# GpSimd's loads in another order, in a kernel for windowed attention and channel mix

## The chip, the cores and the metric

The kernel runs on one core of a Trainium2 chip. The metric is the device time of one execution in microseconds (us), the median of several runs. Five engines work side by side, each through an instruction list of its own: TensorE (PE; PEld are its weight loads), VectorE (DVE), ScalarE (ACT), GpSimd (POOL) and SyncE (SP). Data move by DMA. SP, ScalarE and GpSimd issue DMAs, each on a queue of its own.

## The reference

Eight batches, eight heads, 576 positions, 64 values per head. Causal attention in a window of 128 positions with a linear bias by distance is followed by a channel mix (a feed-forward step with a shift by one position):

```python
scores = q @ k.T / 8 + slope_h * -|i - j|        # masked to 0 <= i - j < 128
x      = softmax(scores) @ v                     # heads side by side: 512 columns
x_prev = x shifted down by one position
xk, xr = mu * x + (1 - mu) * x_prev              # with mu_k and mu_r
out    = sigmoid(xr @ w_r) * (relu(xk @ w_k) ** 2 @ w_v)    # 512 -> 1024 -> 512
```

Inputs and output are float32; the kernel computes in bfloat16 and accumulates in float32.

## The kernel before, in words

All work is written down as nodes of a plan: each has an engine, a duration that the author supposes, dependencies, a priority, the buffers that it takes and gives back, and a function that emits the instruction. `Plan.run` plays the plan through in time. On each engine it takes the ready node with the smallest key that gets its buffers. The order so found is the order in which the instructions are issued. The supposed times decide the order and nothing else; on the chip, an instruction waits for what it really needs, and in each engine's list nothing passes a waiting instruction.

The work on TensorE, by the line numbers of the profile:

- `warm` (L654): 90 matmuls on zeros, with the last priority. They fill TensorE's time at the start when nothing else is ready in the plan.
- q and k are transposed to have the head dimension on partitions: batch 0's first 256 positions from float32 stages (L1097, L1100), the rest with four quarter-array transposes at a time (`qk_quad`, L1053; `halves`, L804). All of them need `ident`, an identity that DVE makes (L408) from `dist`, which GpSimd fills by iota (L404). Two selects on GpSimd (L412, L415) then cut `dist` to the window, and DVE copies it.
- `tails` (L906, L879) does the same for positions 512 to 575.
- `scores` (L693, for batch 0 and the first steps after it with a bias matmul, L680), then exp on ScalarE (L707); later batches multiply by a mask on DVE (L720).
- `attend` (L749) multiplies by v, with a column of ones for the sum; DVE divides (L755, L760).
- The result is transposed back (`out_t` L787, `out_some` L804, for the last two batches by DMA), and `shift` makes xk and xr on DVE (L847, L854).
- `channel_mix`: K (L958, `wk_sb`), relu on ScalarE (L965), the square on DVE (L931) or, in the first three chunks, on DVE or ScalarE (L929), R (L976, `wr_sb`) with a tanh on ScalarE (L983), V (L992, `wv_sb`), the product on DVE (L997), and the store on SP (L1022). The last row block is made in two pieces of 384 and 128 columns; the second is stored by ScalarE (L1016).

The loads: batch 0's first part comes on SP's and ScalarE's queues (`first_load`, L517). All else is loaded and cast to bfloat16 by GpSimd's DMAs, in the order of the text, set by `LOADS = 'vK23tVkabRcWw'` and then by a, b, c for each of the batches 2 to 7. v and V are the halves of batch 0's v, K and k those of w_k, 2 and 3 batch 0's q and k from position 256 on (heads 0 to 3 and 4 to 7), t its tails, R is w_r, W and w are the halves of w_v, and a, b, c are q and k, the tails, and v of a batch. Each of GpSimd's DMAs in the plan depends on the one before it (`last.get(queue)`).

In the plan, each transfer also takes time on one shared resource (`fab`): its bytes by a rate, times a factor by kind (`COST`). Keys of attention nodes come from `rank`: a step number less a lead interpolated from `LEAD`, plus a shift by step kind from `SHIFT`. On TensorE, `pe_key` prefers work of the array shape that is set up, if that is the half-height one (`rows` 64), and can put quarter-array transposes (`lazy`) back by `WAIT`, which is 0.

Of the kernel before, what the change touches and what calls it, by code (L numbers as in the profile page):

```python
# [33 lines left out]
class Plan:  # L34
# [148 lines left out]
def kernel(  # L183
# [14 lines left out]
    B, H, S, D = q.shape  # L198
# [26 lines left out]
    PART_WIDE = True  # L225
    QK1 = (ACT, DVE)
    TW = (0,)
    QUAD = 0.040
# [7 lines left out]
    COST = {'first': 1.28, 'v': 1.15, 'q': 0.944, 'ts': 0.66, 'tv': 0.58, 'w': 0.88, 'run4': 1.0, 'run2': 1.03, 'flip': 1.0, 'mu': 1.0, 'x': 1.0}  # L236
    SS = ()
    OH = range(1, 6)
    QM = 2
# [16 lines left out]
    VDEP = 1  # L256
    TCOST = 1.5
    KLAST = 1

    def XT(b, g):  # L260
        return (ACT,) if b else XT0
# [68 lines left out]
    def dve_t(n, fast=1):  # L330
# [1 line left out]

    AHEAD = 30.0
    LEAD = {
        PE: (46.3, 80.42, 22.29, 25.79, 41.56, 20.38, 22.23, 21.29, 23.26, 26.51),
        ACT: (-27.56, -45.55, 35.23, -5.26, -38.06, -61.17, 26.65, -81.7, -33.31, -34.13),
        DVE: (-18.77, -31.64, -26.58, 23.63, -67.49, 40.6, 13.9, -0.29, -44.69, 6.99),
    }
    KNOTS = range(-4, 36, 4)
    SHIFT = {  # L340
        PE: {(0, 0): 84.89, (1, 0): -15.49, (2, 0): 37.21, (3, 0): 68.05, ('fkk',): -41.42, ('p1', 'fkk'): 6.29, ('p1', 'fxk'): 4.19},
        ACT: {(1, 0): -163.12, (2, 0): 31.31, (3, 0): 165.14, ('frl',): 21.61, ('rl', 'fp1'): 159.69, ('rs', 'fp1'): -160.42},
        DVE: {(0, 0): -143.93, (1, 0): 53.57, (1, 1): -50.21, (1, 2): -15.35, (2, 0): 32.09, (3, 0): -4.67, ('fp1', 'frs'): -48.4, ('frl',): -99.03, ('ot', 'fp1', 'frs'): -1.01},
    }
    NBIAS = 4
    XRL = 4.0
# [1 line left out]
    SLOPE = 4.7  # L348
# [6 lines left out]
    def rank(prio, need, free):  # L355

        if prio[0] == 0:
            _, b, part, g = prio[:4]
            k = 4 * b + g if b or part else g - 4
            step = (prio[4] if len(prio) > 4 else 9, prio[5] if len(prio) > 5 else 0)  # L360
            return {e: ((k - lead(e, min(k, 32))) * SLOPE + SHIFT[e].get(step, 0.0),) + tuple(prio)
                    for e in LEAD}
        if prio[0] == 1:
            what = tuple(sorted(h.cls for h in need)) + tuple(
                "f" + c for c in sorted({h.cls for h in free}))
            return {e: (prio[1] + SHIFT[e].get(what, 0.0),) + tuple(prio) for e in LEAD}
        return {e: (1e9,) + tuple(prio) for e in LEAD}

    def op(e, dur, deps, prio, emit, need=(), free=()):
# [190 lines left out]
    def load_step(what):  # L560
        if what in "vV":
            if what == "v" and VCUT:
                n_w["d"] = pool_op(0.55, emit_cut, [n_ident])
            for j in ((0, 1) if what == "v" else (2, 3)):
                vl[0].append(v_load(0, j, vh[0], [gv[0]] + blank_v + (
                    src0[1, VDEP - 1] if VDEP and j == 0 else [])))
                if j == 0 and not VCUT:
                    n_w["d"] = pool_op(0.55, emit_cut, [n_ident, last[POOL]])
                    last[POOL] = n_w["d"]
            if what == "V":  # L570
                vl[0].append(tv_load(0, vh[0], blank[0:4]))
# [28 lines left out]
    def batch_load(b, what):  # L600
        if what == "a":
            ch[b] = Hold("cb")
            g_ = virtual("cb", [ch[b]])
            if b not in WIDE:
                cl[b] = full_load(b, 0, ch[b], g_) + full_load(b, 1, ch[b], g_)
            else:
                cw[b] = [wide_load(b, ch[b], g_, 4 * j, 4 * j + 4) for j in range(2)]
        elif what == "b":
            th[b], tl[b] = tail_load(b)
            if b in XB:  # L610
                xbh[b] = Hold("qx")
                g_ = virtual("qx", [xbh[b]])
                xbl[b] = [flip(b, i, j, g_) for i in range(2) for j in range(NF)]
            if b in XTT:
                tail_flip(b)
        elif what == "c":
            vh[b] = Hold("vs")
            gv[b] = virtual("vs", [vh[b]])
            vl[b] = [v_load(b, j, vh[b], [gv[b]]) for j in range(NF)]
            vl[b].append(tv_load(b, vh[b]))  # L620

    for what in LOADS:
        load_step(what)
    n_dist, n_wr = n_w["d"], n_w["r"]
    n_wk = [n_w["k", 0], n_w["k", 1]]
    n_wv = [n_w["v", 0], n_w["v", 1]]
    for b in range(2, B):
        for what in "abc":
            batch_load(b, what)

    n_copy = {}
# [260 lines left out]
    def tails(b, prio):  # L892
        htt = Hold("tt")
        hs = th[b]
        if b in XTT:
            plan.follow(last["tt"], ttg[b])
            last["tt"] = ttg[b]
            return tth[b], ttl[b]
        if b not in TW:
            return tails_full(b, prio, htt, hs)  # L900
        hp = Hold("p1")

        def emit(e):
# [8 lines left out]
        t = op(PE, 0.03 * 16, list(tl[b]) + [n_ident], prio + (0,), emit, [hp], [hs])  # L912
        g = virtual("tt", [htt])
# [29 lines left out]
    def channel_mix(P, c0, c1, first, xks, xrs, order):  # L943
# [27 lines left out]
        for i, c in enumerate(range(c0 // 128, c1 // 128)):  # L971
# [30 lines left out]
            for a, b in ((0, FIN), (FIN, 512)) if final else ((0, 512),):  # L1002
# [42 lines left out]
    def qk_quad(b, g, nr, buf, deps, prio, c0, hq, take, free):  # L1045
# [3 lines left out]
        def emit(e):  # L1049
            for n in range(2 * nr):  # L1050
# [8 lines left out]
        t.rows, t.lazy = (64, 64), True  # L1059
# [241 lines left out]
```

## Time and profile before

| | us |
|---|---|
| median of 3 runs (lowest, highest) | 232.38 (231.59, 232.47) |
| the profiled execution | 232.61 |
| its span, first to last instruction | 230.8 |
| TensorE busy | 221.1 (96%) |
| VectorE busy | 186.9 (81%) |
| ScalarE busy | 163.9 (71%) |
| GpSimd busy | 93.7 (41%) |

The granted TensorE clock is full throughout. In lines of the profile, the first number of a timeline row is the start in us, the second its length, and xN the number of instructions that were merged. Of a wait, "A <- B: total, times, longest" says that A stood still until B had ended. For GpSimd, the time of a DMA row is that of its issue, not of the transfer.

### The profile page before, as it was taken

The numbers are of one execution on the slowest core, as the hardware profiler recorded it, in microseconds if no ns is written. First come the engines' busy times: TensorE is split into PE (matmuls) and PEld (weight loads), VectorE is DVE, ScalarE is ACT, GpSimd is POOL, SyncE is SP. The second block draws the span as 40 slices with busy tenths as digits, with TensorE's granted clock in tenths as the row PEclk, the third lists the DMA queues.
The fourth block names the chain that finished last, engine by engine and source line by source line (L and its number), as shares of the span: only waits on it lengthen the run. The fifth ranks groups of instructions, "written<-read, shape, count | busy, mean of one in ns | idle before, by whom it ended". The sixth has DMA issues, their size and how long they took to land.

```text
span 230.8 us, 6660 instructions
## 1 busy us (share of the span) xinstructions
PE 221.1 (96%) x2682; PEld 134.3 (58%) x2715; DVE 186.9 (81%) x422; ACT 163.9 (71%) x296; POOL 93.7 (41%) x120
## 2 busy tenths in 40 slices
PE   7999998899999999999999999999999999999993
PEld 7575765665665755545665755545655654455562
DVE  7495998799977999899769998979999999343342
ACT  3769999489999977898897776964847516417260
POOL 8786655579869950686001990070000000000000
PEclk9999999999999999999999999999999999999999
DMA  6999999999999999989962999499723222121222
GB/s 169 182 163 194 189 158 200 200 167 151 201 147 169 171 125 167 119 82 175 227 98 70 179 151 206 93 122 169 128 57 121 67 82 76 46 92 45 69 70 91
DMA packets 121566, 31.11 MB, mean 135 GB/s; under 512 B 108216, under 2 KB 117696, under 8 KB 121536
## 3 DMA queue, kind: packets, MB, share of 16 engines
q0 software_dynamic: 96016, 16.26, 97.8%
q1 hardware_dynamic: 23776, 13.84, 25.1%
q10 hardware_dynamic: 1744, 0.59, 1.1%
q8 instruction: 21, 0.34, 0.6%
q14 instruction: 9, 0.07, 0.1%
HBM read 33.56 MB, written 9.44 MB: 186 GB/s over the span
## 4 chain that ended last, share of the span: by engine, by line
PE 77%; DMA 16%; issue 2%; POOL 2%; DVE 1%; ACT 1%; DVEq 0%; POOLq 0%; ACTq 0%
PE uno L992 25%; PE uno L958 25%; PE uno L976 12%; DMA wk_sb<-in_moe_w_k_dram 7%; PE duo L749 6%; PE duo L693 5%; DMA cb<-in_k_dram 5%; DMA vs<-in_v_dram 4%; PE uno L804 3%; POOL vs L467 1%; PE uno L1053 0%; DVE dl L847 0%; POOL tv L472 0%; PE uno L879 0%; ACT xt L663 0%
## 5 line engine op out<-in xcount | busy, mean ns | idle before, releaser
L958 PE MATMUL uno<-xk,wk_sb 128*128 128x256 bf16 (+2 forms) x413 | 70.8, 313 | 0.6 <-ACT qk L663 0.4
L992 PE MATMUL uno<-wv_sb,kk 128*128 128x512 bf16 (+2 forms) x282 | 69.5, 373 | 1.9 <-issue 0.8
L707 ACT ACTIVATE at<-duo 128x1024 bf16<-128x1024 f32 (+2 forms) x68 | 65.1, 1002 | 6.1 <-PE duo L693 5.3
L965 ACT ACTIVATE rl<-uno 128x256 bf16<-128x256 f32 (+2 forms) x104 | 47.4, 487 | 30.2 <-PE uno L958 27.0
L958 PEld LDWEIGHTS <-wk_sb 128*128 128x128 bf16 x416 | 38.5, 98 | 22.4 <-issue 0.4
L467 POOL DMA_DIRECT2D vs<-in_v_dram x32 | 28.5, 908 | 45.3 <-PE duo L749 37.2
L992 PEld LDWEIGHTS <-kk 128*128 128x128 bf16 x296 | 27.0, 98 | 27.7 <-issue 1.2
L720 DVE TENSOR_TENSOR at<-at,mask 128x1024 bf16<-128x1024 bf16 x56 | 37.3, 681 | 3.4 <-ACT at L707 3.4
L931 DVE TENSOR_TENSOR kk<-rl 128x256 bf16<-128x256 bf16 (+2 forms) x96 | 30.9, 336 | 9.9 <-ACT rl L965 8.8
L997 DVE SCALAR_TENSOR_TENSOR ot<-rs,uno 128x512 f32<-128x512 bf16 (+2 forms) x37 | 24.4, 667 | 13.8 <-PE uno L992 10.3
L976 PE MATMUL uno<-wr_sb,xr 128*128 128x512 bf16 x128 | 34.3, 379 | 0.8
L983 ACT ACTIVATE rs<-uno 128x512 bf16<-128x512 f32 x36 | 22.2, 628 | 11.7 <-PE uno L976 11.7
L663 ACT COPY qk<-uno 128x512 bf16<-128x512 bf16 (+1 forms) x42 | 22.6, 605 | 5.1 <-PE uno L1053 3.7
L854 DVE SCALAR_TENSOR_TENSOR xr<-dl,mu_sb,xt 128x576 bf16<-128x576 bf16 (+1 forms) x32 | 24.6, 777 | 0.0
L854 DVE SCALAR_TENSOR_TENSOR xk<-dl,mu_sb,xt 128x576 bf16<-128x576 bf16 (+1 forms) x32 | 24.3, 778 | 0.0
L760 DVE TENSOR_TENSOR xu<-duo,rc 128x640 bf16<-128x640 f32 x28 | 22.5, 813 | 2.1 <-PE uno L804 2.1
L749 PEld LDWEIGHTS <-at 128*128 128x128 bf16 x576 | 21.1, 98 | 5.1 <-issue 0.5
L976 PEld LDWEIGHTS <-xr 128*128 128x128 bf16 x144 | 13.6, 98 | 14.2 <-issue 0.2
L498 POOL DMA_DIRECT2D cb<-in_q_dram x20 | 17.7, 916 | 5.6 <-PE uno L804 3.2
L749 PE MATMUL duo<-vs,at 128*128 128x65 bf16 x448 | 18.7, 194 | 0.1
L498 POOL DMA_DIRECT2D cb<-in_k_dram x20 | 17.7, 916 | 2.2 <-PE uno L804 1.6
L663 ACT COPY xt<-uno 128x640 bf16<-128x640 bf16 (+3 forms) x28 | 15.1, 580 | 3.8 <-PE uno L804 2.4
(83 smaller groups left out, 200.3 us busy)
## 6 DMA issues: line engine op xcount, KB each, us to landing
out_dram<-ot SPq DMA_DIRECT2D x30, 256.0 KB, 4.1
vs<-in_v_dram POOLq DMA_DIRECT2D x32, 128.0 KB, 7.0
cb<-in_q_dram POOLq DMA_DIRECT2D x20, 128.0 KB, 6.1
cb<-in_k_dram POOLq DMA_DIRECT2D x20, 128.0 KB, 5.5
out_dram<-ot SPq DMA_DIRECT2D x10, 128.0 KB, 1.8
wk_sb<-in_moe_w_k_dram POOLq DMA_DIRECT2D x2, 512.0 KB, 7.5
cb<-in_q_dram POOLq DMA_DIRECT2D x4, 256.0 KB, 10.0
cb<-in_k_dram POOLq DMA_DIRECT2D x4, 256.0 KB, 10.4
```

Of the source, the lines that this page charges most:

```text
L467: return dma(POOL, 256, issue_t(1024), lambda e: nc.gpsimd.dma_start(out=vs_buf[h.idx][:, j, :, 0:D], in_=v[b, :, 128 * j:128 * j + 128].r ...
L498: return [dma(POOL, 256, issue_t(1024), lambda e, r=r: nc.gpsimd.dma_start(out=cb_buf[h.idx][:, i, r], in_=src[:, :, r]), [g], kind="q") f ...
L663: (nc.scalar.copy if e == ACT else nc.vector.tensor_copy)(out=out, in_=in_)
L707: lambda e, ah=ah, w=w, hp=hp: nc.scalar.activation(out=ah(), in_=two(hp)[:, :, 0:w], func=AF.Exp, scale=float(scale)), (), [hp])
L720: nc.vector.tensor_tensor(out=a, in0=a, in1=m, op=ALU.mult)
L749: nc.tensor.matmul(a[:, hl, t - t0], lhsT=at[:, lo:lo + 128], rhs=vs[:, u, 2 * g + hl, :] if u < NF else tvb[:, 2 * g + hl], start=(u == u ...
L854: lambda e: nc.vector.scalar_tensor_tensor(out=buf[hk.idx][:, g, e0 + c0:e0 + c1], in0=dls(), scalar=mu[:, g:g + 1], in1=xc(1), op0=ALU.mu ...
L931: nc.vector.tensor_tensor(out=out, in0=in_, in1=in_, op=ALU.mult)
L958: nc.tensor.matmul(one(hp)[:, 0:n], lhsT=wk_sb[:, po, 128 * fo:128 * fo + 128], rhs=xk_buf[hx.idx][:, po, c0:c1], start=(po == 0), stop=(p ...
L965: a = op(ACT, act_t(n), [s], pr, lambda e, hp=hp, hr=hr: nc.scalar.activation(out=rl_buf[hr.idx][:, 0:n], in_=one(hp)[:, 0:n], func=AF.Rel ...
L976: nc.tensor.matmul(one(hp), lhsT=xr_buf[hx.idx][:, po, 128 * c:128 * c + 128], rhs=wr_sb[:, po], start=(po == 0), stop=(po == NPO - 1))
L992: nc.tensor.matmul(one(hv)[:, a:b], lhsT=kk_buf[hk.idx][:, fo, o:o + 128], rhs=wv_sb[:, fo, a:b], start=(fo == 0), stop=(fo == NFO - 1))
```

## The change

The change keeps every instruction's work and moves instructions. `order` means the issue order on an engine.

1. GpSimd's DMAs no longer depend on each other in the plan (`PFREE`). Each gets a key: its place in the text plus a number for its group (`PKEY`; the group is the batch and the letter). A load whose buffer is not free yet lets later ones pass. The iota and the selects take part in this, with their place as key.
2. In the plan, the transfer of 37 early loads takes a time of its own from a table (`LAND`), in place of bytes by rate.
3. `rank` adds shifts for batches 0 and 1 by step (`FIRST`), by head pair (`PAIR`) and by what a feed-forward node takes and gives (`MIX`); `LEAD`, `SHIFT` and `QUAD` have new numbers, and `WAIT` is 13.59.
4. `pe_key` tells three array shapes apart in place of one: 64 (scores), 63 (`qk_quad`) and 127 (`tails`).
5. The five row blocks whose store is issued in two halves begin one block earlier: the last but one is stored whole (`CUTOFF`).
6. Tail loads of v name the hold of v as a dependency.

In the new program GpSimd's list begins: q of heads 0 to 3 ('2'), the two tail loads ('t'), k of heads 0 to 3, both loads of 'v', 'K', then the iota, q of heads 4 to 7 ('3'), the two selects, k of heads 4 to 7, 'V', then 'a' and 'b' mixed, 'R', 'k', three loads of 'c', 'W', the other two of 'c', batch 2's first load, 'w', batch 2's other three, four tail loads, and so on. Of the filler matmuls, 58 stand ahead of the first real one (30 before) and 32 behind it. ScalarE's list has 7 squares more.

```diff
     def pe_key(self, n, rows):
         key = n.prio["PE"] if isinstance(n.prio, dict) else n.prio
-        if rows == 64 and n.rows[0] == 64:
+        if rows < 128 and n.rows[0] == rows:
             return (-1e8,) + tuple(key)
...
-    WAIT = 0.0
+    WAIT = 13.59
...
+    LAND = {
+        '0v1': 1.03, '0K0': 2.27, '020': 0.73, '021': 0.77, '030': 0.75, '031': 0.9, '0t0': 0.75,
...
+    CUTOFF = 2
+    PFREE = True
...
+            def at(e):
+                s = (k - lead(e, min(k, 32))) * SLOPE + SHIFT[e].get(step, 0.0)
+                if b < 2:
+                    s += FIRST[e].get((b, part) + step, 0.0) + PAIR[e].get((b, part, g), 0.0)
+                return s
+            return {e: (at(e),) + tuple(prio) for e in LEAD}
...
-        us *= COST.get(getattr(n, "kind", None), 1.0)
+        us = LAND.get(getattr(n, "load", None), us * COST.get(getattr(n, "kind", None), 1.0))
...
+    PKEY = {
+        '0v': -8.52, '0K': -7.98, '02': -0.25, '03': -25.82, '0t': -61.35, '0V': -5.2, '0k': 6.38,
...
     def dma(queue, kb, issue, emit, deps=(), need=(), free=(), lat=(1.0, 0.9), flip=False, kind='x'):
-        n = plan.add(queue, issue, 0.0, list(deps) + [last.get(queue)],
-                     (len(plan.nodes),), emit, need)
+        free_ = PFREE and queue == POOL
+        n = plan.add(queue, issue, 0.0, list(deps) + ([] if free_ else [last.get(queue)]),
+                     (PKEY.get(group[0], 0.0) + place[0], len(plan.nodes)) if queue == POOL else (len(plan.nodes),),
+                     emit, need)
...
     def pool_op(dur, emit, deps=()):
-        n = plan.add(POOL, dur, 0.2, list(deps) + [(last.get(POOL), 0.0)],
-                     (len(plan.nodes),), emit)
+        n = plan.add(POOL, dur, 0.2, list(deps) + ([] if PFREE else [(last.get(POOL), 0.0)]),
+                     (place[0] - 0.5, len(plan.nodes)), emit)
...
-                        cut = (a, 256, b) if 0 < B * S - 128 - row <= 128 * n_split else (a, b)
+                        cut = (a, 256, b) if 128 * CUTOFF <= B * S - 128 - row < 128 * (n_split + CUTOFF) else (a, b)
```

More of the change, by code (lines that the diff above doesn't have):

```diff
@@ L227 @@
     TW = (0,)
-    QUAD = 0.040
+    QUAD = 0.035
     RUN = {2: 64 * 284 / 345.0, NF: 128 * 284 / 390.0}
@@ L234 @@
     NO = 5
-    WAIT = 0.0
-    COST = {'first': 1.28, 'v': 1.15, 'q': 0.944, 'ts': 0.66, 'tv': 0.58, 'w': 0.88, 'run4': 1.0, 'run2': 1.03, 'flip': 1.0, 'mu': 1.0, 'x': 1.0}
+    WAIT = 13.59
+    COST = {
+        'first': 1.28, 'v': 1.15, 'q': 0.94, 'ts': 0.66, 'tv': 0.58, 'w': 0.88, 'run4': 1.0, 'run2':
+        1.03, 'flip': 1.0, 'mu': 1.0, 'x': 1.0,
+    }
+    LAND = {
[6 rows of a table added]
+    }
     SS = ()
@@ L340 @@
     SHIFT = {
-        PE: {(0, 0): 84.89, (1, 0): -15.49, (2, 0): 37.21, (3, 0): 68.05, ('fkk',): -41.42, ('p1', 'fkk'): 6.29, ('p1', 'fxk'): 4.19},
-        ACT: {(1, 0): -163.12, (2, 0): 31.31, (3, 0): 165.14, ('frl',): 21.61, ('rl', 'fp1'): 159.69, ('rs', 'fp1'): -160.42},
-        DVE: {(0, 0): -143.93, (1, 0): 53.57, (1, 1): -50.21, (1, 2): -15.35, (2, 0): 32.09, (3, 0): -4.67, ('fp1', 'frs'): -48.4, ('frl',): -99.03, ('ot', 'fp1', 'frs'): -1.01},
+        PE: {
+            (0, 0): 99.96, (1, 0): 4.2, (2, 0): 27.32, (3, 0): 102.83, ('fkk',): -6.62, ('p1',
+            'fkk'): 0.33, ('p1', 'fxk'): -1.01,
+        },
+        ACT: {
+            (1, 0): -298.05, (2, 0): 77.7, (3, 0): 214.26, ('frl',): -106.04, ('rl', 'fp1'): 54.43,
+            ('rs', 'fp1'): -149.39,
+        },
+        DVE: {
+            (0, 0): -148.98, (1, 0): 70.65, (1, 1): -77.21, (1, 2): -53.91, (2, 0): 78.03, (3, 0):
+            0.86, ('fp1', 'frs'): -66.8, ('frl',): -42.09, ('ot', 'fp1', 'frs'): -49.77,
+        },
+    }
+    FIRST = {
+        PE: {
[3 rows of a table added]
+        },
+        ACT: {
+            (0, 0, 3, 0): -12.01, (0, 0, 2, 0): -1.6, (0, 0, 1, 0): 1.62, (0, 1, 3, 0): 10.66, (0,
+            1, 2, 0): -19.23, (0, 1, 1, 0): 49.91, (1, 0, 3, 0): -27.16, (1, 0, 2, 0): 30.91, (1, 0,
+            1, 0): -23.81,
+        },
+        DVE: {
[4 rows of a table added]
+        },
+    }
+    PAIR = {
+        PE: {
[3 rows of a table added]
+        },
+        ACT: {
[3 rows of a table added]
+        },
+        DVE: {
[6 rows of a table added]
+        },
+    }
+    MIX = {
+        PE: {
+            (0, 'p1', 'fxk'): 63.56, (0, 'p1', 'fkk'): -28.77, (0, 'fkk'): -13.61, (1, 'p1', 'fxk'):
+            -14.46, (1, 'p1', 'fkk'): -12.63, (1, 'fkk'): -45.13,
+        },
+        ACT: {
+            (0, 'rl', 'fp1'): 16.16, (0, 'frl'): -36.53, (0, 'rs', 'fp1'): -32.31, (1, 'rl', 'fp1'):
+            -35.06, (1, 'frl'): -9.5, (1, 'rs', 'fp1'): -83.25,
+        },
+        DVE: {
+            (0, 'frl'): 52.11, (0, 'ot', 'fp1', 'frs'): 55.27, (1, 'ot', 'fp1', 'frs'): -26.97, (1,
+            'frl'): 8.37,
+        },
     }
@@ L365, in rank @@
                 "f" + c for c in sorted({h.cls for h in free}))
-            return {e: (prio[1] + SHIFT[e].get(what, 0.0),) + tuple(prio) for e in LEAD}
+            return {e: (prio[1] + SHIFT[e].get(what, 0.0) + (
+                MIX[e].get((prio[2] // 14,) + what, 0.0) if prio[2] < 28 else 0.0),) + tuple(prio)
+                    for e in LEAD}
         return {e: (1e9,) + tuple(prio) for e in LEAD}
@@ L390, in fab @@
         return x
-    def dma(queue, kb, issue, emit, deps=(), need=(), free=(), lat=(1.0, 0.9), flip=False, kind='x'):
-        n = plan.add(queue, issue, 0.0, list(deps) + [last.get(queue)],
-                     (len(plan.nodes),), emit, need)
+    PKEY = {
[5 rows of a table added]
+    }
+    group, place = [""], [0.0]
+    def dma(queue, kb, issue, emit, deps=(), need=(), free=(), lat=(1.0, 0.9), flip=False, kind='x'):
+        free_ = PFREE and queue == POOL
+        n = plan.add(queue, issue, 0.0, list(deps) + ([] if free_ else [last.get(queue)]),
+                     (PKEY.get(group[0], 0.0) + place[0], len(plan.nodes)) if queue == POOL else (len(plan.nodes),),
+                     emit, need)
+        if queue == POOL:
+            place[0] += 1
+            n.group = group[0]
+            n.load = group[0] + str(sum(1 for x in plan.nodes if getattr(x, 'group', None) == group[0]) - 1)
         n.kind = 'flip' if flip else kind
@@ L619, in batch_load @@
             vl[b] = [v_load(b, j, vh[b], [gv[b]]) for j in range(NF)]
-            vl[b].append(tv_load(b, vh[b]))
+            vl[b].append(tv_load(b, vh[b], [gv[b]]))
     for what in LOADS:
+        group[0] = "0" + what
         load_step(what)
@@ L628 @@
         for what in "abc":
+            group[0] = str(b) + what
             batch_load(b, what)
```

13 lines of the change are left out of this document (6 added, 7 removed), and 28 rows, old and new, of tables (FIRST, LAND, PAIR, PKEY).

## The prediction

> **What bounds the kernel now.** First the page. Its PE line says that TensorE is busy for 221.1 of 230.8 us, so a better order can win only the rest, plus what TensorE does without need. Second, TensorE's waits, once whole and once from 53 us on:
>
> ```profile
> PE uno L654 <- DVE warm L434: 1.0, 1, 1.0
> PE uno L992 <- DMA wv_sb<-in_moe_w_v_dram: 0.7, 1, 0.7
> PE duo L680 <- ACT at L707: 0.5, 1, 0.5
> PE uno L958 <- ACT qk L663: 0.4, 1, 0.4
> PE uno L1097 <- DMA qx<-in_q_dram: 0.3, 1, 0.3
> PE uno L1053 <- DMA cb<-in_k_dram: 0.3, 1, 0.3
> PE uno L1100 <- ACT qk L663: 0.2, 1, 0.2
> PE uno L1053 <- ACT qk L663: 0.2, 1, 0.2
> PE uno L749 <- ACT xt L663: 0.2, 1, 0.2
> ```
>
> After 53 us the same view holds one line, 0.6 us in four pieces of 0.2. So a rearranged middle can win at most 0.6 us; what can be won lies ahead of 53 us and behind TensorE's end (227.3). Third, the timeline of TensorE's first microseconds, and GpSimd's beside it:
>
> ```profile
> 0.99 3.27 PE L654 MATMUL uno<-warm 128*128 128x128 bf16 x30 [0.99 <-DVE warm L434]
> 4.10 0.56 PE L1100 MATMUL uno<-ident,qx 128*128 128x128 bf16 x4
> ```
> ```profile
> 0.84 0.34 POOL L404 IOTA dist<- 128x256 bf16 x1 [0.39 <-POOLq L1285]
> ...
> 2.22 2.00 POOL L467 DMA_DIRECT2D vs<-in_v_dram  x2
> 4.21 0.76 POOL L508 DMA_DIRECT2D wk_sb<-in_moe_w_k_dram  x1
> 4.96 0.76 POOL L463 DMA_DIRECT2D qx<-in_q_dram  x1
> 5.69 0.77 POOL L463 DMA_DIRECT2D qx<-in_k_dram  x1
> ...
> 7.89 0.67 POOL L482 DMA_DIRECT2D ts<-in_q_dram  x1
> 8.52 0.65 POOL L482 DMA_DIRECT2D ts<-in_k_dram  x1
> ```
>
> Real work begins at 4.10. It needs `ident`, which DVE makes from the iota that GpSimd finishes at 1.18. The 90 filler matmuls (L654) do no work. Fourth, ScalarE: the table of stretches has it busy 10.00 of 10 us from 30 to 40, and then it idles:
>
> ```profile
> 39.75 1.02 ACT L707 ACTIVATE at<-duo 128x1024 bf16<-128x1024 f32 x1
> 43.91 1.56 ACT L663 COPY qk<-uno 128x512 bf16<-128x512 bf16 x3 [3.14 <-PE uno L1053]
> ```
>
> It waits for transposes of batch 2, and these for k of batch 2 (landed 43.5). The page's DMA row is full over the first 40 us. The front is thus shared between loads and ScalarE.
>
> **What TensorE loses ahead of 53 us now.** 0.99 at the start, 3.3 for 30 fillers, 60 x 0.056 = 3.4 for the later ones (13 of them took 0.89 us, the last one's 0.22 included), and the waits of the list without its first line, 2.8: together 10.5 us.
>
> **1. The start.** In the instruction order of the new program GpSimd issues, ahead of the iota, one q load of part 2, the two tail loads, one k load, two v loads and half of wk. From the first free moment of GpSimd (0.84) and start to start: 2 x 0.73 (4.96 to 5.69) + 2 x 0.64 + 2.00 + 0.75 = 5.5, so the iota starts at 6.3. From the iota's start to that of `ident` are 0.57 (0.84 to 1.41), and `ident` takes 0.13: the first real transpose stands at 7.1 instead of 4.10, **3.0 us late**. On DVE three casts of first loads now stand ahead of `ident`; the last wants k of head pair 1, which landed at 4.6, so 2 us may go before that decides. Queued behind the iota are one more q load and the two selects; with 0.73 and 0.64 they end at 8.1, and the distance copies on DVE by 8.5. The first bias matmul (L680) is due then: 7.1 + transposes 2 x 0.33 + 12 fillers 0.7 = 8.4. So this costs nothing more.
>
> The fillers stand 58 ahead of that transpose and 32 behind it (30 and 60 before). The 58 end at 0.99 + 3.3 + 28 x 0.056 = 5.9 and TensorE then idles 1.2. The later ones cost 32 x 0.056 = 1.8 instead of 3.4. New loss: 7.1 + 1.8 = **8.9 us plus its waits w**. Without any wait that wins 1.6 us; w = 1.6 is the break-even.
>
> **2. The loads.** GpSimd's stream begins 1.4 us earlier (0.84 instead of 2.22). Its data do not begin as soon: in the DMA view of the first 5 us only SP's and ScalarE's queues move data (0.80 MB), and GpSimd's have no packet, although its first load was issued at 2.22. So the stream gains between 0.4 us (it has to share with the first loads, and delays them) and 1.4 (it does not). The row is that no packet was seen while the other two queues were full. [...]
>
> wv's first half, which ended the 0.7 us wait, now has batch 1's last v block and v tail behind it instead of ahead: 384 KB at the 180 to 190 GB/s of the table of stretches, 2.0 us. It lands 2.4 to 3.4 us earlier, near 34.5. Batch 2's second load keeps the same set ahead and gains 0.4 to 1.4 (near 42.5), while 36 AV matmuls, 8 of K, 4 of V and 20 output transposes are put ahead of its first transposes: 36 x 0.031 + 8 x 0.109 + 4 x 0.216 + 0.4 = 3.2 us more of other work. The DMA waits (0.7, 0.3, the 0.3 of the first loads) and the 0.4 behind the batch 2 copy go: **1.7 off the waits**, and ScalarE's 3.14 us hole mostly closes.
>
> **3. What is late next: ScalarE.** It starts 3 us later. Of batch 0's and 1's first three feed-forward chunks it gets 7 more squares (0.32 each back to back, 43 to 37 and 29 to 28 on DVE) two 512-wide copies less (0.48) and one 256-wide more (0.31): +1.6 us. To offset that it had about 4 us of idle time between 4.69 and 15.7, of which the earlier part 2 fills some, and the 3.14 hole. The four ScalarE waits above were 1.1 us (0.5 + 3 x 0.2). Bounds for w: 0 (they are filled as well) and 4 (a 3 us late start and 1.6 more work, less the 0.6 or so that could be filled at once). I take 1.0, by the row it is nearest to, the four waits of now. Front: 8.9 + 1.0 - 10.5 = **-0.6**.
>
> **4. The middle.** In both programs TensorE changes its array shape 118 times and runs the same matmuls, so new keys and the two new modes only permute. Later batches' tail loads go ahead of v and of q, k. Batch 3's q and k landed at 59.2, their first transposes ran at 62.2: about 3 us of cover against two tail loads pulled ahead (1.2 us each at 47 us). Value 0, between -0.6 (the list) and +1.5 (cover gone).
>
> **5. The stores.** The halved stores move forward by one row; the last but one goes whole.
>
> ```profile
> 226.34 1.40 DVE L997 SCALAR_TENSOR_TENSOR ot<-rs,uno 128x512 f32<-128x512 bf16 x3 [3.45 <-PE uno L992]
> ```
>
> Now two halves are issued at 227.06 and 227.44, which holds SP until 227.9; the last row's 384 columns (ready at 227.5) are issued at 227.96 and land 1.96 later. One whole store takes SP 0.33 and lands after 2.0 (the two at 203 and 205 us). The 384 columns then leave at 227.55: **-0.4**, and no more, since ScalarE's last store lands at 229.5 anyway.
>
> **Sum.** -0.6 + 0 - 0.4 = -1.0. The profiled execution took 232.61 us (span 230.8 and 1.8 around it), 0.23 above the median of 232.38; it gives 231.6, so 231.4 against the median.
>
> **Rivals.** *Faster: the stalls vanish.* w = 0 to 0.4, because the earlier part 2 and batch 2 fill ScalarE: -1.6 to -1.2 in front, -0.4 at the end, up to -0.6 in the middle: 229.8 to 230.8, with 230.3 in its midst. For it: ScalarE's 3.14 us hole and its idle early microseconds. Against: the 3 us late start is lost for ScalarE as well.
> *Slower: ScalarE becomes the bound of the front.* Place: the exps (L707) of batch 0's second part up to the squares of the third chunk, some 18 to 45 us. It decides once TensorE's waits for it exceed 1.6 + 0.4 + 1.2 = 3.2 us before 53 us. For it: 10.00 of 10 us busy now. At w = 4: +2.4 - 0.4 = +2.0, 234.4.
> *The loads were not the bound.* If the order on TensorE, not the landing, set the DMA waits (they follow each other in a full stream), they return at the next load: w = 1.0 + 1.7, +1.1 - 0.4, so 233.1. For it: the stream's total to 45 us is unchanged and gains only 0.4 to 1.4.
>
> **Chances.** A measurement here tells about 0.5% (1.16 us), so the forecast itself counts as no change, with its edges at 231.2 and 233.5. The forecast with its neighbours up to the third rival: 0.36; stalls vanish: 0.36; slower beyond 0.5%, by ScalarE or both: 0.28. Range: from 230.0, just above the floor of the first rival, to 234.2, just short of w = 4. The likeliest case's own range is 231.2 to 232.6.
>
> **What would show it.** The first L1100 matmul near 7.1 with 58 fillers ahead; the L992 wait for wv gone; ScalarE without a hole near 40 us; TensorE's waits before 53 us, the first 7.1 left out, 1.0 in sum; 231.4 - 232.38 split as -0.6 in front and -0.4 behind TensorE's end. It is wrong if the iota comes earlier than 6, if waits after 53 us exceed 1.5, or if ScalarE's waits in front pass 3.

## The result, and the profile after

| | before | after |
|---|---|---|
| median (lowest, highest), 16 runs each, us | 232.36 (231.59, 234.50) | 234.35 (233.75, 235.71) |
| ratio, 95% interval | 1 | 1.0073 (1.0053 to 1.0092) |
| the profiled execution, and its span, us | 232.61, 230.8 | 234.21, 232.3 |
| end of TensorE's last matmul, us | 227.34 | 229.09 |
| last store landed, us | 229.92 | 231.39 |

The change makes the kernel 0.7% slower. The forecast was 231.4; the result lies 0.15 us above the range. In the profiled executions TensorE ends 1.75 us later, and the stretch behind its end is 0.28 shorter (2.30 in place of 2.58). They differ by 1.60 us, the medians by 1.99, so 0.4 us of the result is not in what the traces show.

TensorE's waits of the changed kernel, the whole list (waited for: total, times, longest):

```profile
PE uno L1199 <- DVE ident L504: 1.1, 1, 1.1
PE uno L752 <- DVE warm L530: 1.0, 1, 1.0
PE duo L778 <- ACT at L805: 0.4, 1, 0.4
PE uno L1152 <- issue: 0.4, 1, 0.4
PE uno L1057 <- ACT xt L761: 0.3, 1, 0.3
PE duo L791 <- DVE xu L858: 0.2, 1, 0.2
PE duo L847 <- ACT at L805: 0.2, 1, 0.2
PE uno L1075 <- ACT rl L1064: 0.2, 1, 0.2
PE uno L885 <- ACT qk L761: 0.2, 1, 0.2
PE uno L1057 <- ACT qk L761: 0.2, 1, 0.2
```

Every wait for a DMA is gone from this list, as forecast, and yet the kernel is slower. That is the lesson of the case: a wait can vanish because the load comes earlier, or because TensorE comes later. The start on TensorE, and GpSimd's:

```profile
0.99 5.40 PE L752 MATMUL uno<-warm 128*128 128x128 bf16 x58 [0.99 <-DVE warm L530]
7.50 0.38 PE L1199 MATMUL uno<-ident,qx 128*128 128x128 bf16 x4 [1.11 <-DVE ident L504]
...
8.94 0.48 PE L778 MATMUL duo<-dist,sid 128*128 128x384 bf16 x2
...
10.33 0.44 PE L1004 MATMUL uno<-ident,ts 128*64 128x64 bf16 x16
```
```profile
1.25 0.92 POOL L559 DMA_DIRECT2D qx<-in_q_dram  x1 [0.80 <-POOLq L1384]
...
6.00 0.77 POOL L604 DMA_DIRECT2D wk_sb<-in_moe_w_k_dram  x1
6.84 0.39 POOL L500 IOTA dist<- 128x256 bf16 x1
7.13 0.79 POOL L559 DMA_DIRECT2D qx<-in_q_dram  x1
```

The first real transpose stands at 7.50, not 4.10. ScalarE near 40 us has no hole of 3.14 us any more, but one of 0.91:

```profile
42.72 0.82 ACT L1064 ACTIVATE rl<-uno 128x256 bf16<-128x256 f32 x2
43.57 0.42 ACT L1028 ACTIVATE kk<-rl 128x256 bf16<-128x256 bf16 x1
44.90 1.18 ACT L761 COPY xt<-uno 128x640 bf16<-128x640 bf16 x2 [0.91 <-PE uno L902]
```

And at 162 us VectorE stands for a tile whose store has not landed:

```profile
162.35 0.69 DVE L1096 SCALAR_TENSOR_TENSOR ot<-rs,uno 128x512 f32<-128x512 bf16 x1 [1.05 <-DMA out_dram<-ot]
```

To place the 1.75 us, each TensorE instruction's start is compared with the work ahead of it. Fillers count nothing, and every other matmul has one price for its shape, its usual step from start to start in the trace of after (an estimate for the small shapes): 0.216 us for 512 columns, 0.163 for 384, 0.109 for 256, 0.056 for 128, 0.031 for 65, 0.117 for a float32 transpose, 0.060, 0.034 and 0.023 for 256, 128 and 64 columns at half height, 0.023 for a batch 0 tail, and 0.0155 for a quarter-array transpose. The trace of before lacks the records of 33 matmuls of 512 columns; their weight loads are in it and give their places. The difference of start and work is the lag, in us:

| useful work done, us | 2 | 6 | 8 | 12 | 16 | 20 | 30 | 50 | 140 | 160 | end |
|---|---|---|---|---|---|---|---|---|---|---|---|
| before | 6.09 | 9.76 | 10.29 | 12.05 | 12.29 | 12.62 | 14.62 | 14.90 | 15.18 | 15.53 | 15.82 |
| after | 8.90 | 10.46 | 11.84 | 13.30 | 14.35 | 14.44 | 15.71 | 16.20 | 16.38 | 17.20 | 17.57 |
| after, iota and selects first | 8.23 | 9.62 | 10.99 | 12.45 | 13.67 | 13.77 | 14.86 | 15.35 | 15.54 | 16.04 | 16.40 |
| after, three repairs | 7.96 | 9.34 | 10.71 | 11.70 | 13.17 | 13.61 | 14.69 | 15.17 | 15.36 | 15.80 | 16.16 |
| after, three repairs, all masks early | 7.43 | 8.81 | 10.19 | 11.17 | 12.37 | 13.26 | 14.34 | 14.82 | 15.01 | 15.45 | 15.82 |

The kernels named after share one order on TensorE, so their rows differ by the same at any prices. Between before and after the order differs, and with the median or the mean step as price the differences move by up to 0.6; those at 2 us of work and at the end hardly do.

Of the 2.8 us of late start, as they stand at 2 us of work, 0.7 is left at 6 us of work, since up to there the old kernel waits and runs more fillers. From there to 16 us of work (real time is work and lag together, so some 16 to 30 us) the difference grows to 2.1. By 50 us of work the changed kernel has won back 0.8 of it. Behind that it loses 0.45 in all, between 140 and 160 us of work, where the wait at 162 us stands.

### The profile page after: what moved, and what is told of

It is laid out like the page before. It is cut to its first block, busy times and chain, and to the rows that moved or that the text cites. A ratio compares the mean times of both kernels' runs of the same rounds, so it can differ in the third digit from the quotient of the medians.

```text
span 232.3 us, 6704 instructions
## 1 busy us (share of the span) xinstructions
PE 224.7 (97%) x2715; PEld 135.4 (58%) x2715; DVE 187.5 (81%) x416; ACT 165.3 (71%) x302; POOL 93.5 (40%) x120
## 3 DMA queue, kind: packets, MB, share of 16 engines
q0 software_dynamic: 96016, 16.26, 100.4%
## 4 chain that ended last, share of the span: by engine, by line
PE 83%; DVE 5%; ACT 4%; DMA 3%; POOL 2%; issue 2%; DVEq 0%; POOLq 0%
PE uno L1057 26%; PE uno L1091 25%; PE uno L1075 12%; PE duo L791 7%; PE duo L847 6%; PE uno L902 3%; DMA out_dram<-ot 3%; PE uno L1152 2%; PE duo L778 1%; ACT at L805 1%; PE uno L847 1%; DVE ot L1096 1%; POOL qx L559 1%; ACT qk L761 1%; DVE xu L858 1%
## 5 line engine op out<-in xcount | busy, mean ns | idle before, releaser
L1091 PE MATMUL uno<-wv_sb,kk 128*128 128x512 bf16 (+2 forms) x296 | 71.5, 374 | 0.1
L1057 PE MATMUL uno<-xk,wk_sb 128*128 128x256 bf16 (+2 forms) x416 | 69.9, 314 | 0.4 <-ACT xt L761 0.3
L818 DVE TENSOR_TENSOR at<-at,mask 128x1024 bf16<-128x1024 bf16 x56 | 36.7, 681 | 3.6 <-ACT at L805 3.4
L1075 PE MATMUL uno<-wr_sb,xr 128*128 128x512 bf16 x144 | 36.7, 379 | 0.2 <-ACT rl L1064 0.2
L1082 ACT ACTIVATE rs<-uno 128x512 bf16<-128x512 f32 x36 | 22.3, 624 | 19.5 <-PE uno L1075 16.6
L1030 DVE TENSOR_TENSOR kk<-rl 128x256 bf16<-128x256 bf16 (+2 forms) x89 | 28.8, 338 | 8.9 <-ACT rl L1064 7.5
L761 ACT COPY qk<-uno 128x512 bf16<-128x512 bf16 (+1 forms) x41 | 21.1, 589 | 6.8 <-PE uno L1199 3.7
```

The source lines that it names most:

```text
L761: (nc.scalar.copy if e == ACT else nc.vector.tensor_copy)(out=out, in_=in_)
L818: nc.vector.tensor_tensor(out=a, in0=a, in1=m, op=ALU.mult)
L1030: nc.vector.tensor_tensor(out=out, in0=in_, in1=in_, op=ALU.mult)
L1057: nc.tensor.matmul(one(hp)[:, 0:n], lhsT=wk_sb[:, po, 128 * fo:128 * fo + 128], rhs=xk_buf[hx.idx][:, po, c0:c1], start=(po == 0), stop=(p ...
L1075: nc.tensor.matmul(one(hp), lhsT=xr_buf[hx.idx][:, po, 128 * c:128 * c + 128], rhs=wr_sb[:, po], start=(po == 0), stop=(po == NPO - 1))
L1091: nc.tensor.matmul(one(hv)[:, a:b], lhsT=kk_buf[hk.idx][:, fo, o:o + 128], rhs=wv_sb[:, fo, a:b], start=(fo == 0), stop=(fo == NFO - 1))
```

## The experiments

Ratios are to the kernel before, with the 95% interval. The edits move instructions in the order of emission, or leave out fillers. "Before" or "after" is the kernel that was edited.

**1. Was it the late iota?** Three variants of after: the iota and `ident` moved to the front of the emission order; that without 28 of the 58 leading fillers; that with the selects in front as well.

```diff
-        for n in plan.run():
+        order = [n for n in plan.run() if n.emit is not None]
+        front = [n_iota, n_warm, n_ident]            # third variant, and later: + n_dist
+        order = front + [n for n in order if n not in front]
+        fill = [n for n in order if n in warms][:28] # second and third variant
+        order = [n for n in order if n not in fill]
```

> The changed kernel with the iota and the making of ident moved to the front of GpSimd's and DVE's lists; every other list is as it was. Theory L (the late iota is paid in full): the first real transpose moves from 7.5 us to the end of the 58 fillers, 6.4, and the kernel gains 1.1: ratio to before 1.0025. Theory S (the early loads delay each other: the tail load landed at 10.05 and the last first load at 10.4, and the matmuls that want them ran at 10.33 and 10.70): TensorE arrives earlier and waits there, gain at most 0.3: ratio 1.006.

> As a_iota_first, and 28 of the 58 leading fillers left out, so that 30 stand ahead of the first transpose as in the kernel before. Theory L: first transpose near 4.6, gain 2.9 over the changed kernel, ratio 0.995. Theory S: the new waits at the tails (L1004 line) and at the float32 transposes grow by what the start gains; gain at most 0.3, ratio 1.006.

> As a_iota_first_30, and the two selects moved ahead of GpSimd's first load as well, so that its loads are issued from about 2.2 us on, as in the kernel before. Theory S: SP's and ScalarE's first loads land by 7.8 again instead of 10.4, the tails by about 9.3 instead of 10.05; gain over the changed kernel 0.8 to 1.2, ratio 1.003. Theory L: no better than a_iota_first_30, since GpSimd's stream begins 1 us later: ratio 0.997.

Measured: 1.0063 (1.0038 to 1.0088), 1.0134 (1.0102 to 1.0165), 1.0039 (1.0014 to 1.0064). With the iota alone the transpose comes at 6.67, then the bias matmul waits 0.49 us for the distance copies. With 28 fillers fewer the transpose is back at 4.17, as early as before, and the kernel is slower still. TensorE's start in that second variant, and its stretches (length, busy times with counts of PE, PEld, DVE, ACT and POOL, granted clock, DMA share, GB/s):

```profile
4.17 0.63 PE L1200 MATMUL uno<-ident,qx 128*128 128x128 bf16 x4
...
8.44 0.48 PE L779 MATMUL duo<-dist,sid 128*128 128x384 bf16 x2 [1.90 <-DVE dist L731]
...
10.40 1.97 PE L1197 MATMUL uno<-id,qx 128*128 128x128 f32 x8
```
```profile
8.00:10.00 2.00, 1.56 (x18) 0.61 (x19) 1.46 (x9) 0.76 (x2) 1.71 (x4) 0.95 2.14 167
10.00:11.00 1.00, 1.00 (x19) 0.94 (x18) 0.93 (x8) 0.75 (x2) 1.00 (x3) 0.50 1.81 186
11.00:12.00 1.00, 1.00 (x7) 1.00 (x6) 0.70 (x4) 0.44 (x1) 1.00 (x2) 0.50 1.28 207
12.00:13.00 1.00, 1.00 (x12) 0.74 (x14) 0.59 (x1) 0.14 (x1) 0.96 (x2) 0.50 1.30 200
```

The selects stand behind eight loads still, so 1.90 us of waiting follow, and then the granted clock is 0.50 for 3.4 us (9.8 to 13.2): the float32 transposes take 1.97 us, against 1.09 at a clock of 1.00 in the third variant. With all 58 fillers, in the first variant, the wait is 0.49 us and the mean clock of the profiled execution 0.999, against 0.990 here. So the fillers are of use here, though they compute nothing. The third variant shows what is next:

```profile
4.17 0.58 PE L1200 MATMUL uno<-ident,qx 128*128 128x128 bf16 x4
...
9.13 0.75 PE L1005 MATMUL uno<-ident,ts 128*64 128x64 bf16 x16 [1.55 <-DMA ts<-in_q_dram]
```

The tail load, which landed at 9.1, sets the pace. A start 3.3 us earlier wins 0.8 to 1.2 us. One more variant tells whether that gain is the start's or the loads': iota, `ident` and selects first, and all 58 fillers kept.

> The changed kernel with the iota, ident and the two selects first, and all 58 leading fillers kept. Theory S: TensorE reaches the tails near 9.4 instead of waiting 1.5 us for them as without the 28 fillers; the time is that of a_cut_first_30, ratio 1.004. Theory L: the transposes at 6.4 instead of 4.2 cost 2 us more: ratio 1.012.

Measured: 1.0042 (1.0013 to 1.0071). The first transpose is at 6.43, 2.3 us later than with 30 fillers, and the time is the same. So when TensorE starts does not matter between 4.2 and 6.4 us; the landing at 9 us does. What these two variants win, 0.7 to 0.8 us by the ratios and 0.85 (with all fillers) by the lag at 8 us of work, comes either from distances that are ready earlier, or from GpSimd's stream that starts at 2.10 and not at 1.25, so that the last first loads land at 8.6 to 9.1 and not at 10.2 and 10.4. These runs do not tell the two apart.

**2. The wait at 162 us.** After, with the output tiles taken in turn and not by lowest number:

```diff
+        if h.cls == "ot" and free:
+            return min(free, key=lambda a: (self.freed.get(a, -1), a))
...
+        if h.cls == "ot":                          # when a tile is given back
+            self.freed[h.idx] = len(self.freed) + max(self.freed.values(), default=0)
```

> The changed kernel with the five output tiles used in turn (the one freed longest ago) instead of the lowest free one; the order of instructions is the same. Theory O: the 1.05 us wait of DVE for a store at 162 us goes, and with it 0.5 us of the loss at the scores of batch 7: ratio 1.005. Rival: that wait is covered or comes back at another store: ratio 1.007.

Measured: 1.0068 (1.0041 to 1.0094). VectorE's wait for the store is gone and the lag at 160 us of work falls from 17.20 to 16.93. That is 0.27 us in the trace, too little for a ratio to tell.

**3. The load order alone, in before.** The first 31 loads of before in after's order; then also the first seven of them ahead of the iota.

```diff
+        new = [pool_loads[i] for i in [3, 7, 8, 4, 0, 1, 2, 5, 6, 9, 10, ...]]
+        for i, n in zip(at, new):                  # at: where the 31 loads stand in the order
+            order[i] = n
+        front = [n_warm] + blank_v + new[:7]       # second kernel only
+        order = front + [n for n in order if n not in front]
```

> The kernel before with its first 31 GpSimd loads in the changed kernel's order (iota and selects still first); all other lists untouched. If the new load order is the good part: the wait for wv (0.7) and those at batch 2 (0.3 and 0.4) shrink and the kernel gains 0.5 to 1.4: ratio 0.994 to 0.998. Rival: that order fits only the changed kernel's TensorE list; here v lands later (11 to 13 us instead of 8 to 9) while the attention of the first part waits for it, and w_r comes no earlier: ratio 1.000 to 1.004.

> As b_load_order, with the first seven of these loads ahead of the iota, as in the changed kernel. Theory L (late iota paid in full): the first transpose moves from 4.1 to 7.5, and as this kernel has only 30 fillers ahead of it, TensorE idles: 2.5 to 3.4 over b_load_order, ratio near 1.012. Theory S (the start is not what bounds; TensorE stands and fills in the first 15 us anyway): below 1.0 over b_load_order.

Measured: 1.0202 (1.0148 to 1.0257) and 1.0221 (1.0180 to 1.0263). TensorE's two longest waits in the first of these and, below them, the longest in the second:

```profile
PE uno L962 <- DMA wk_sb<-in_moe_w_k_dram: 2.8, 1, 2.8
PE uno L753 <- DMA vs<-in_v_dram: 1.1, 1, 1.1
...
PE uno L1104 <- DVE qx L667: 5.4, 1, 5.4
```

The order that serves after starves before, whose TensorE list wants w_k and v earlier. In the second, TensorE waits 5.4 us for its first cast, and the waits for w_k and v are gone. That the ratios are nearly alike does not say that this wait is free: in each of the two, four of the six runs show a lower granted clock (0.986 to 0.993), and the first's two runs at full clock took 235.3 and 235.9 us, its other four 237.3 to 238.2. The two traces have the same order on TensorE and a mean clock of 0.999 or more, so they can be compared: the second is 5.4 us behind at 2 us of work and 1.1 from 16 us of work to the end. Most of the late start is absorbed by the waits behind it, not all.

**4. Does ScalarE bound the front?** After, with five of the eight mask exps (L1238) moved into ScalarE's pauses at 9 to 13 us:

```diff
+        early = {acts[5].seq: ms[0:2], acts[8].seq: ms[2:5]}   # exps behind ScalarE's steps 5 and 8
+        gone = [n for m in early.values() for n in m]
+        order = [x for n in order if n not in gone for x in [n] + early.get(n.seq, [])]
```

> The changed kernel with five of ScalarE's eight mask exps moved from 20 to 27 us into its idle time at 9 to 13 us; all other lists untouched. Theory A (ScalarE, which began 3.2 us later, bounds TensorE between 17 and 30 us): 1.0 to 1.5 gained, ratio 1.001 to 1.003. Rival (TensorE is held by something else there, DVE or loads): below 0.3, ratio 1.006.

Measured: 1.0069 (1.0041 to 1.0096). The lag at 12 us of work falls by 0.5, but at 25 by only 0.4, and the time by nothing that the ratio shows.

**5. The square completed, two controls, three repairs.** After with the loads in the order of before (iota first); before with the new store cut only; before with six mask exps early; after with iota and selects first, output tiles in turn and five mask exps early. The first puts the loads into the order of the text, the second takes one line of the change, the others use the edits shown (in before the six exps stand behind ScalarE's steps 7, 8 and 10).

```diff
+        for i, n in zip(at, pool_loads):           # first kernel: at as above, the order of the text
+            order[i] = n
-                        cut = (a, 256, b) if 0 < B * S - 128 - row <= 128 * n_split else (a, b)
+                        cut = (a, 256, b) if 256 <= B * S - 128 - row < 128 * (n_split + 2) else (a, b)
```

> The changed kernel's lists on TensorE, ScalarE, VectorE and SyncE, but on GpSimd the iota, the selects and the first 31 loads in the order of the kernel before. With the three kernels that had the iota first it completes a square: lists of before with loads of before (ratio 1), lists of before with loads of after (1.0202), lists of after with loads of after (1.0042). Theory M (each list fits only the loads that it was planned with): the changed lists wait for loads that now land later than planned, the two v loads and w_v's halves above all (first half of w_v near 37.4 in place of 36.4, part 2's second pair of q and k, wanted early by the changed list); DMA waits of 1.5 us or more appear and the ratio is 1.010 or more. Theory S2 (the changed lists are slower by themselves, the loads are not what matters for them): DMA waits under 0.6 us and a ratio of 1.002 to 1.007, near that of the kernel with the iota first. Theory G (GpSimd's stream is the loss): 0.998 to 1.001.

> The kernel before with only the halved stores one row block earlier, the last but one stored whole; only SyncE's list differs. By the prediction's step 5 the end of the span behind TensorE's end falls from 2.58 us to 2.2, -0.4 us, ratio 0.998 to 0.999 (the comparison can hardly tell it from 1; the trace's last landings tell it). Rival: the whole store of the last but one row keeps the data queues busy longer than its halves did, the last two stores land as late as before, and nothing is won.

> The kernel before, with six of ScalarE's eight mask exps moved from about 16 to 30 us into its idle time at 8 to 12 us; only ScalarE's order differs. Theory A (ScalarE is what the front of the kernel before waits for: busy 10 of 10 us from 30 to 40): 6 x 0.3 = 1.8 us of its work leave the full stretch, TensorE's waits for it (1.1 us) fall by half or more, -0.5 to -1.0 us, ratio 0.996 to 0.998. Theory D (the loads of w_v and batch 2 wait behind it and take back what is won): the ScalarE waits fall, the waits for w_v and batch 2 grow by as much, ratio 0.999 to 1.001.

> The changed kernel with three repairs at once: iota and selects ahead of all loads (-0.8 us alone), output tiles used in turn (-0.5 alone), five mask exps in ScalarE's idle time at 8 to 13 us (-0.2 alone). Theory I (the repairs sit at different places: first 10 us, 12 to 27 us, 162 us): they add, -1.3 to -1.5, 232.9 to 233.1, ratio 1.001 to 1.003. Theory O (they free the same slack, or the next wait takes it): no better than the best of them, 233.5, 1.004.

Measured: 1.0656 (1.0619 to 1.0692), 1.0003 (0.9977 to 1.0028), 1.0001 (0.9977 to 1.0025), 1.0004 (0.9978 to 1.0030). The first holds an accident (GpSimd stood 5.72 us behind VectorE's fill of the v tiles) and is tried again below. With the new store cut, before ends 2.42 us behind TensorE's end in place of 2.58; its profile also held a wait of 0.8 us for a transposing DMA at 160 us, which has nothing to do with the cut. With its masks early, before gains nothing: the listed ScalarE waits shrink from 1.5 to 1.1, the wait for w_v stays (0.8), and ScalarE is busy 9.86 of 10 us from 30 to 40 us still. Its TensorE lag is 0.4 us below the old kernel's at 30 us of work; a wait of 0.67 us at 52.3 us, which the old list did not have and whose cause the profile does not show, takes that back and more. And the three repairs of after together win 1.6 us: level with before.

**6. What is left between the two.** Between 12 and 18 us of work the repaired kernel loses more than 1 us against the old one. There `qk_quad` waits 0.78 us at 28.8; the profile names no cause, but the copy ahead of it on ScalarE ends at 28.5 and stands behind a mask exp. Earlier, the last 12 fillers take 0.8 us from 16.8 on. So: all eight exps early; without the 12 fillers; both.

```diff
+        early = {acts[5].seq: ms[0:2], acts[8].seq: ms[2:5], acts[30].seq: ms[5:6], acts[33].seq: ms[6:7], acts[36].seq: ms[7:8]}
+        fill = [n for n in order if n in warms][-12:]
+        order = [n for n in order if n not in fill]
```

> The changed kernel with the three repairs (iota and selects first, output tiles in turn, five mask exps early) and, beside them, the other three mask exps moved out of the place in front of batch 1's qk copies at 27 us into ScalarE's pauses at 21.6 and 22.8 us and behind the next copy. In the run with the three repairs TensorE's lag behind the kernel before was nothing at 16 us of work and 0.8 at 18 to 20, where a wait of 0.78 us for a copied pair of transposes stands at 28.8. Theory Q (that copy is late because the mask stands ahead of it on ScalarE): the wait falls to 0.4 or less, -0.3 to -0.5 us, ratio 0.997 to 0.999. Theory U (ScalarE is full there whatever the order; the exps moved ahead make the next thing late, xt or the exp at 22): no change, 1.000 to 1.002, with waits for xt or exps grown by 0.3.

> The changed kernel with the three repairs, without the last 12 of the 90 filler matmuls on zeros, which stand between output transposes at 16.8 to 17.7 us and take 0.9 us of TensorE there. Theory F (fillers that stand among real work late in the front cost what they take): -0.4 to -0.8 us, ratio 0.997 to 0.999. Theory H (they cover waits for VectorE's divided tiles and for transposed pairs, which come no earlier): waits of 0.5 us or more stand in their place, -0.2 to +0.1, ratio 0.999 to 1.001.

> Both of the edits above in one: the changed kernel with the three repairs, all eight mask exps early and without the last 12 fillers. If Q and F hold they add, -0.7 to -1.3 us against the three repairs alone: 231.4 to 232.0, ratio 0.995 to 0.998, faster than both kernels. If either of U and H holds, 0.997 to 1.000; if both, 1.000 to 1.002.

Measured: 1.0008 (0.9991 to 1.0025), 0.9998 (0.9970 to 1.0026), 0.9982 (0.9959 to 1.0005). In the first, the wait falls from 0.78 to 0.48 and the loads take the rest back, since w_k's second half now ends a wait:

```profile
27.93 0.26 PE L1158 MATMUL uno<-ident,cb 64*64 64x64 bf16 x9 [0.48 <-issue]
28.16 1.90 PE L1081 MATMUL uno<-wr_sb,xr 128*128 128x512 bf16 x7
30.68 0.61 PE L1063 MATMUL uno<-xk,wk_sb 128*128 128x256 bf16 x4 [0.63 <-DMA wk_sb<-in_moe_w_k_dram]
```

Without the 12 fillers a wait of 0.33 us for VectorE's `xu` stands in the place of 0.8 us of fillers. Both together, 232.15 us, are the lowest median of all, and beat after with intervals that do not touch. That they beat before is not shown: the interval reaches 1.0005.

**7. The square's last corner, mended.** The fill of the v tiles ahead of the first v load:

```diff
-        front = [n_iota, n_warm, n_ident, n_dist]
+        front = [n_iota, n_warm, n_ident, n_dist] + blank_v
```

> The same as the kernel with the old load order before it (lists of after, iota, selects and the first 31 loads in the old order), with the zero-fill of v's tiles on VectorE ahead of the first v load: in the first try GpSimd stood 5.72 us before its second load, since the fill of v's tiles waited for the first load to land, and the 1.0656 measured there holds that accident. Theory M (the changed lists fit only their own load order): TensorE wants the tails near 10.3, and in the old order they land at 16.0 and 16.5: a wait of 5 to 6 us at the tails, little of it made up later, ratio 1.018 to 1.027. Theory S2 (the lists would bear it like a late start, which cost half or less): 1.004 to 1.012.

Measured: 1.0413 (1.0363 to 1.0462), more than either theory gave. TensorE's rows, and a stretch and the page's clock row:

```profile
8.47 0.34 PE L795 MATMUL duo<-qk 64*128 64x256 bf16 x4
16.26 0.42 PE L1008 MATMUL uno<-ident,ts 128*64 128x64 bf16 x8 [7.45 <-DMA ts<-in_q_dram]
...
17.22 1.97 PE L1200 MATMUL uno<-id,qx 128*128 128x128 f32 x8
```
```profile
18.00:20.00 2.00, 2.00 (x28) 1.74 (x26) 0.86 (x2) 0.59 (x1) 1.28 (x2) 0.50 1.27 190
20.00:22.00 2.00, 2.00 (x24) 0.45 (x12) 0.42 (x1) 0.95 (x2) 1.42 (x3) 0.50 1.44 197
```
```profile
PEclk9956999999999999999999999999999999999999
```

The changed list wants the tails at 8.8; in the old order they land at 16.2. The wait of 7.45 us is followed by some 6 us of work at a granted clock of 0.50 (16.3 to 22.3), about 3 us more (an estimate, from these 6 us and the 1.97 us of the float32 transposes in place of 1.09). TensorE ends at 237.47, 9.5 later than with the new loads (227.93). All with the iota first, the square reads:

| | loads of before | loads of after |
|---|---|---|
| lists of before | 1 | 1.0202 |
| lists of after | 1.0413 | 1.0042 |

Lost clock is part of both high entries: all six runs of the 1.0413 show 0.977 to 0.986, and four of the six of the 1.0202 as said above (its two others lie 1.3% above before). Either way neither half of the change can be judged alone: order of loads and lists of the engines are one plan.

## Why the prediction was wrong, point by point

**The start** was right in kind: 58 fillers, an idle stretch (1.2 forecast, 1.11 measured), then the transpose, at 7.50 instead of 7.1. GpSimd's first load came at 1.25, not 0.84, and that is the 0.4. The 58 fillers ended at 6.39, not 5.9, which the wait for `ident` hid. The sum priced 28 of them at 0.056, but the first 39 step by 0.107, up to 5.19 us, where the trace's first clock record stands (1.00), and by 0.056 from there on. In the old kernel the same change comes at 4.01. That the clock is full throughout, as was said of the kernel before, is thus not shown for its start: no clock record stands ahead of 4.01 there and 5.19 here, and up to these times the same matmuls step by 0.107 in place of 0.056. What I did not see is how little a start is worth here: of 2.8 us, 0.7 is left at 6 us of work, and between 4.2 and 6.4 us the start moves nothing. A late start and the landing of the first and tail loads are alternatives, and the later one decides; the step priced the start alone.

**The loads** failed as a step, and one other failure follows from it. The stream was to gain 0.4 to 1.4 us. At batch 2's last q and k load, the same set of loads done, it had gained 0.17 (45.59 against 45.76); the lower end of 0.4 was the author's estimate, and no run shows it. w_v's first half landed at 36.44, not at 34.5: w_k's second half stood directly behind w_r and landed 3.1 us after it, while in before it had landed 1.7 us after the load ahead of it. The first V matmul starts at 37.58, against 37.44 before, with 12 K matmuls fewer done. So "1.7 off the waits" came true, but not because data came sooner: TensorE arrived later. The rival that the loads were not the bound had seen half of it; it expected the DMA waits to return, and they did not.

The stream shared the DMA engines with the first loads and delayed them, as the lower end had it. In the first 5 us GpSimd's queue moved 0.08 MB and the other two 0.55, in place of none and 0.80, and the last two first loads on each of SP's and ScalarE's queues landed at 8.2 to 10.4 us, in place of 6.1 to 7.8. Their transposes ran from 10.70, in place of 7.01.

**ScalarE**: w was set at 1.0 and the list shows 1.9 us of waits between the first transpose and 53 us, 1.5 of them for ScalarE. But the list holds only the larger waits. Counting every gap up to 55 us, waits for DMA fell from 2.1 to about 0.2, those for ScalarE rose from 3.3 to 3.6 and those for VectorE, `ident`'s apart, from about 0.2 to 1.0. So waits fell by 0.8 and not by 1.8: this is the term that was mis-sized most. I took the four waits that the list showed for the whole, and they were a third of ScalarE's. The rival with ScalarE as the bound gave 234.4, almost the time measured, but not for its reason: its condition, waits for ScalarE over 3.2 us ahead of 53 us, was not met in the list (1.5); counted with every gap they are 3.6, but 3.3 in the old kernel already. Moving five exps out of the way won nothing that the ratio shows.

**The middle** was put at 0, between -0.6 and +1.5, and cost 0.45 behind 50 us of work (0.25 to 0.6, by the prices used). A wait of 1.05 us for an output store on VectorE is part of it: without it TensorE's end came 0.27 earlier.

**The stores** won 0.28 in after and 0.16 in before with the cut alone, not 0.4. ScalarE's small store of the last row was said to land at 229.5 anyway; in after it is the last to land (231.39), 0.23 behind SP's.

**The sum**: front +1.3 for -0.6 (of the 1.9 between them, 0.4 by the start, 1.0 by waits; the other 0.5 is not placed, and no run here told its parts apart), middle +0.45 for 0, stores -0.28 for -0.4. So the steps that failed are the two behind "1.7 off the waits" and w = 1.0: the loads came 0.17 earlier and not 0.4 to 1.4, and the waits left over were sized by a list of the larger ones. None of the three signs named for being wrong came up: the iota stood at 6.84, the listed waits behind 53 us were 0.2, and ScalarE's listed waits in front 1.5.

**What was shown and what was not.** Shown: putting iota and selects first, the output tiles in turn and five masks early, together, brings the changed kernel level with the old one; each alone is at the edge of what a ratio tells. In the traces, one execution each, TensorE's end comes 1.17, 0.27 and 0.43 us earlier by each alone, and 1.41 by all three, of the 1.75. Shown: the new lists need the new load order, and the old lists lose by it. Not settled: which of the new keys makes the stretch from 16 to 30 us slower. Two sites in it were found, a mask exp ahead of a copy and fillers among real work; mended together they are worth 0.6 us of median, with an interval as wide.

## What to carry to other kernels

When a wait is gone from the list, look whether what was awaited came earlier or the engine that waited came later; the landing times tell, the list of waits does not. An engine's late start is not a term to add in full, since the next true dependency (here a load at 9 us) swallows part of it: 0.7 of 2.8 us was left here, and 1.1 of 5.4 in the old kernel with the new load order. Compare the lag at several amounts of work done, and see whether the comparison stands with other prices. A load order that was searched together with the engines' lists can't be valued, kept or carried over without them.

## What the runs showed of the hardware

- The granted TensorE clock was lower after two of the pauses seen here and not after a third. In the second variant of experiment 1, TensorE waited 1.90 us for the distances, until 8.44; with TensorE at work again, the clock was 0.50 from 9.8 to 13.2 us. In experiment 7, around the wait of 7.45 us that ended at 16.26, it was 0.50 from 12 to 22.3 us, 6 us of it after work had begun again. A pause of 1.55 us (third variant of experiment 1), 7.58 to 9.13, left it at 1.00 in the profiled execution, while three of the twelve runs of that kernel show 0.990 to 0.993. What decides between these cases was not shown.
- The same 512 KB load of w_k's second half landed 1.7 us after the load ahead of it in one order and 3.1 us in another, so the landing times of the one order did not hold in the other.
